# Four token blocks of a feed-forward part taken as two of 512 tokens, with their x fetched earlier and output products moved ahead

## The chip, the cores and the metric

One Trainium2 chip, one of its cores. The metric is the time on the device of one execution, in microseconds (us). Before the change it is 745.0 us, the median of 3 runs (744.06 to 746.33).

## The reference

Three parts, one after the other, on 2304 tokens (4 sequences of 576) of width 512. Cut to what matters here:

```python
# 1: attention in a window of 64 keys, 8 heads of 64
# 2: a dense feed-forward part, 512 -> 2048 -> 512
h = x @ w_in
sp = np.where(h > 20.0, h, np.log1p(np.exp(np.minimum(h, 20.0))))
g = h * np.tanh(sp)
x = g @ w_out
# 3: each token to one expert of 8, 512 -> 1024 -> 512
logits = x @ w_gate + modality_bias[modality_id]
e_idx = np.argmax(logits, axis=1)
...
for e in range(E):
    mask = e_idx == e
    h = np.maximum(x[mask] @ w1[e], 0.0)
    out[mask] = gate_w[mask, None] * (h @ w2[e])
```

The change is in part 2, and in what hands its rows on to part 3.

## The kernel before

**Tiles.** Part 2 takes the tokens in 9 blocks of 256. Every operand of a product is split into a rounded high part and a low part (hi + lo), and a product is three: hi x hi, lo x hi, hi x lo. `hidden` (line 341) makes 256 of the 2048 hidden features for one block: 2 halves of 128 features, 4 slices of the width, 3 products, so 24 TensorE products of 256 columns (tokens) into one bank of `h`. `mish_a`, `mish_b` and `split_g` turn `h` into `g`: on ScalarE a tanh (line 425), a square (426), an exp (427), a scaled copy (428), another square (436) and the rounded copy of g (444); on VectorE lines 430, 437, 438 and the low part of g (445). `output` (380) multiplies g with `w_out`: 12 products of 512 columns (features of the result) into the two banks of `acc`, one for each 128 tokens.

**The list of steps.** `steps` holds one entry for each step: ("m", block, feature group) for part 2, then ("s", slot, group) for expert slots of 256 tokens. The position i in it is used throughout: 0 to 15 are blocks 0 and 1, 16 to 23 block 2, then 8 positions for each block, 64 to 71 for block 8, and slots from 72. The loop at line 1221 writes out the order of every engine's queue by hand. In position i: the hidden products of i; the end of the activations of i-1 (`finish_mish`); a call of `run_tasks`; splits and fetches of x; the output products of i-2 (`LAG` is 2); the start of the activations of i (`start_mish`, its four ScalarE instructions); the split of g of i-1 (`finish_split`); a second call of `run_tasks`; and, where a block has ended, the copy of its two banks of `acc` into SBUF rows (`keep_rows`, a stash of 4 pairs). Up to position 27 attention's steps are woven in (`att_a`, `att_b`): products for scores and transposes behind the hidden products, products with v at the end.

**x.** Blocks from 2 on get x from DRAM: `fetch_x` (393) issues two transfers on SP in the fifth step of the block before; `split_x` (400) makes hi (ScalarE, line 407) and lo (VectorE, line 408), two instructions each, one step later. xh and xl have two buffers each, so the next block's x is written while the present one is read.

**Routing.** From position 28 on each `run_tasks` call takes one small task from a list. For each block there are 8 with two dot products each on VectorE (line 560), one that chooses the expert, an empty one, and one that places the rows: small TensorE products (line 611 and on), short VectorE instructions, and two scatters of rows to DRAM on POOL (line 639). Blocks are routed in order, 11 calls each, two calls a step; block 8 in a shorter form. When block 6 has been placed, two gathers on POOL (line 890) for the first slot follow, one in each of the second and third next call; position 71 transposes these rows on TensorE (`turn`, line 913).

Of the kernel before, what the change touches and what calls it, by code (L numbers as in the profile page):

```python
# [11 lines left out]
F32 = mybir.dt.float32  # L12
F32R = mybir.dt.float32r
BF16 = mybir.dt.bfloat16
I32 = mybir.dt.int32
# [24 lines left out]
PRE = 12  # L40
AHEAD = 1
MASK_PE = 26
PT_ACT = range(5, 27)
RAW_AT = -1, 1, 3
V_AT = 1
# [233 lines left out]
class Rounds:  # L279


    def __init__(self, nc, ctx, tc, a):
        self.nc, self.tc, self.ctx = nc, tc, ctx
        self.a = a
        self.c = {}
        self.s1, self.s2, self.x01 = [], [], {}
# [54 lines left out]
    def hidden(self, w, xh, xl):  # L341
# [49 lines left out]


    def fetch_x(self, b):
        self.xraw = []
        for i in range(2):
            t = self.x_pool.tile([P, 2, G], F32, name="xraw")
            self.nc.sync.dma_start(t, self.a["x"][b, :, 2 * i : 2 * i + 2])
            self.xraw.append(t)

    def split_x(self):  # L400

        nc = self.nc
        xh = self.xs_pool.tile([P, KD, G], F32R, name="xh")
        xl = self.xs_pool.tile([P, KD, G], F32R, name="xl")
        for i in range(2):
            to = slice(2 * i, 2 * i + 2)
            nc.scalar.copy(xh[:, to], self.xraw[i])
            nc.vector.tensor_tensor(xl[:, to], self.xraw[i], xh[:, to].bitcast(F32), ALU.subtract)
        return xh, xl

    def first_x(self, b):

        if b not in self.x01:
            self.x01[b] = (
                self.xs_pool.tile([P, KD, G], F32R, name="xh"),
                self.xs_pool.tile([P, KD, G], F32R, name="xl"),
            )
        return self.x01[b]

    def mish_a(self, h):  # L420
# [39 lines left out]
    def route_consts(self):  # L460
# [15 lines left out]
        tmp = room("row0")  # L476

        def iota(name, n, step, base=0, cm=0, dt=F32):
            i = p.tile([P, n], I32, name=name + "_i")
# [23 lines left out]
        def bias():  # L503
            n = NT // P
            mod = tmp(2 * n).bitcast(I64)
            nc.sync.dma_start(mod, self.a["mod"])
            mf = tmp(n)
            nc.vector.tensor_copy(mf, mod.bitcast(I32).rearrange("p (n t) -> p t n", t=2)[:, 0])
            b = p.tile([P, NM, NE], F32, name="brow")
# [12 lines left out]
            c["bias"] = bias  # L522
# [19 lines left out]

        return first, bias, last

    def keep_rows(self, acc, pool):

        rows = [pool.tile([P, ROW], F32, name=f"row{c}") for c in range(2)]
        for c in range(2):
# [357 lines left out]
    def turn(self, rows):  # L906
        nc = self.nc
        xh = self.xs_pool.tile([P, KD, G], F32R, name="xh")
        xl = self.xs_pool.tile([P, KD, G], F32R, name="xl")
# [33 lines left out]
def tile_kernel(tc, a):  # L943
    nc = tc.nc
    with ExitStack() as ctx:
# [7 lines left out]
        c0_pool = pool("consts", 1)  # L953
        R.w1_pool = pool("w1", 8)
        R.w2_pool = pool("w2", 8)
        R.xs_pool = pool("xsplit", 2)
        R.m_pool = pool("mish", 2)
        R.m1_pool = pool("mish1", 1)
        R.g_pool = pool("g", 3)
        c = R.c  # L960
        c["ident"] = c0_pool.tile([P, P], F32, name="ident")
        make_identity(nc, c["ident"])
# [5 lines left out]
        with tc.manual_schedule():  # L968
# [136 lines left out]
            gs, accs, xsp = {}, {}, {}  # L1105

            NS = EARLY + STRAIGHT
            steps += [("m", b, j) for b in range(2, NG) for j in range(FP)]
# [28 lines left out]
            def route_block(b, r):  # L1137
# [6 lines left out]
                tasks.append([choose])  # L1144
                if b in REST:
                    tasks.append([])
                tasks.append([weigh, place])
                routed.append(b)
                if len(routed) == PICK_AFTER + 1:
                    tasks[-1].append(R.pick)  # L1150
# [15 lines left out]

                    tasks.extend(([both], [], [others]))

            routed = []

            def out_step(i):
                if i < 0:
                    return
                part, b, j = steps[i]
                if j == 0:
                    accs[part, b] = new_acc(1 if b == NS - 1 else 2)
                last = (FP if part == "m" else FS) - 1
# [6 lines left out]
                if part == "s":  # L1184
                    R.finish(acc, rows.pop(b))
                else:
                    ended.append((b, acc))

            kept, waiting, late, ended = [], [], [], []
            pend, mish = None, None  # L1190
            end_convert = CONV_END
            n = len(steps)
# [13 lines left out]

            def start_mish():
                nonlocal mish
                if part == "m":
                    mish = R.mish_a(h)  # L1210

            def run_tasks():
# [8 lines left out]
            for i in range(n + LAG):  # L1221
                part, b, j = steps[i] if i < n else (None, None, None)
                if i == end_convert:
                    assert not todo and not half_done and not low_parts
                    early.close()
                    R.stash_pool = pool("stash", 4, side="right")
                    R.x_pool = pool("xraw", 2, side="right")
                if part == "m":
                    assert {("in", j, 0), ("in", j, 1)} <= ready
                if part:  # L1230
                    xh, xl = R.x01[b] if part == "m" and b < 2 else xsp[part, b]
                    if b < NS - 1:
                        h = R.hidden(R.w1[j] if part == "m" else ew1[b, j], xh, xl)
# [8 lines left out]
                if part == "s" and b < NS - 1:  # L1242
                    gs[i] = R.relu(h)
                turning = i >= TURN_AT
                if not turning:
                    run_tasks()
                if part == "m":
                    nxt = 2 if i == end_convert else b + 1 if b >= 2 and j == 4 else None
                    if nxt is not None and nxt < NG:
                        R.fetch_x(nxt)  # L1250
                    nxt = 2 if (b, j) == (1, FP - 1) else b + 1 if b >= 2 and j == 5 else None
                    if nxt is not None and nxt < NG:
                        xsp["m", nxt] = R.split_x()
                    if b == NG - 1:
                        if j == 0:
                            e0 = nc.values_load(
# [6 lines left out]
                            ew1[0, j - 6] = R.split_w1(j - 6)  # L1263
                        if j == 7:
                            assert len(rows[0]) == 2
                            xsp["s", 0] = R.turn(rows[0])
                            R.stage_tile(2)
                            R.fetch_w(e0, None, 2, 0)
                if part == "s" and b + 1 < EARLY and j == 1:
                    xsp["s", b + 1] = R.turn(rows[b + 1])  # L1270
                if part == "s" and j == 3 and EARLY <= b + 1 < NS:
                    xsp["s", b + 1] = R.turn(rows[b + 1])
# [49 lines left out]
            for s in range(STRAIGHT, NSLOT):  # L1322
# [8 lines left out]
                xh, xl = R.turn(r)  # L1331
                acc = new_acc()
                g = {}
                for k in range(FS + 1):
# [42 lines left out]
```

## Time and profile before

| | |
|---|---|
| median of 3 runs | 745.0 us (744.06 to 746.33) |
| the profiled execution | 745.39 us, of which 743.7 us from its first to its last instruction (span) |
| mean granted TensorE clock | 0.995 |
| DMA, mean over the span | 102 GB/s |
| positions 24 to 55 (blocks 3 to 6) | 229.63 to 415.98 us of the span |
| positions 56 to 71 (blocks 7 and 8) | 415.98 to 507.42 us |

Times of rows are us from the start of the span. In the timeline a row is start, duration, engine, line of the kernel, operation, out <- in, shape (partitions x elements), count, and in brackets the idle time of the engine before it with what released it. PE is TensorE, DVE VectorE, ACT ScalarE, POOL GpSimd, SP SyncE. TensorE products overlap, so what one costs in a run is the distance from its start to the next start, not its duration.

### The profile page before, as it was taken

To read this page: it belongs to the slowest core of one execution; us is meant where nothing else is said; L and a number is where in the kernel's file an instruction comes from. 1 tells how busy PE (TensorE), PEld (TensorE's weight loads), DVE (VectorE), ACT (ScalarE), POOL (GpSimd) and SP (SyncE) were. 2 spreads that over 40 slices of the span, in tenths; PEclk is the share of its full clock that TensorE was granted. 3 is DMA by queue.
4 is the path that set the end of the run, shared out by engine and by line. 5 is a ranking of instruction groups with operands and counts; after the bars stand their busy time and mean duration, and the time that the engine had idled before them with its cause. 6 is when DMAs were issued, how large, how long until landed. Compare 5 with 4: busy or idle time off the path is not lost. (4 is left out here: it accounts for less than half of the span.)

```text
span 743.7 us, 14036 instructions
## 1 busy us (share of the span) xinstructions
PE 719.8 (97%) x5123; PEld 648.3 (87%) x5123; DVE 558.7 (75%) x1316; ACT 496.4 (67%) x1036; POOL 154.5 (21%) x291
## 2 busy tenths in 40 slices
PE   5789999999999999999999999999999999999996
PEld 4678889889889899989998899998999999999995
DVE  4879999965565489888998898999987556545660
ACT  4978888888776677777767777776324546545462
POOL 4752232233223010100101001031123012220111
PEclk9999999999999999999999999999999999999998
DMA  9987677532332300100101000361012711110520
GB/s 263 308 237 220 198 239 225 183 107 79 94 109 70 128 31 1 49 10 30 58 1 58 1 30 29 114 172 56 30 57 72 255 43 58 57 44 29 200 85 33
DMA packets 42913, 75.51 MB, mean 102 GB/s; under 512 B 3858, under 2 KB 20242, under 8 KB 42707
## 3 DMA queue, kind: packets, MB, share of 16 engines
q1 hardware_dynamic: 30818, 56.01, 24.0%
q0 software_dynamic: 4480, 14.46, 5.7%
q10 hardware_dynamic: 7536, 4.06, 1.9%
q8 instruction: 42, 0.69, 0.4%
q14 instruction: 37, 0.30, 0.1%
HBM read 82.36 MB, written 13.39 MB: 129 GB/s over the span
## 5 line engine op out<-in xcount | busy, mean ns | idle before, releaser
L348 PE MATMUL h<-xh,w 128*128 128x256 f32 x576 | 166.8, 290 | 0.7 <-DVE y L438 0.7
L351 PE MATMUL h<-xl,w 128*128 128x256 f32 x576 | 163.5, 284 | 0.0
L352 PE MATMUL h<-xh,w 128*128 128x256 f32 x576 | 163.5, 284 | 0.0
L387 PE MATMUL acc<-w,g 128*128 128x512 f32 x288 | 115.6, 401 | 0.0
L348 PEld LDWEIGHTS h<-xh,w 128*128 128x128 f32 x576 | 110.9, 193 | 5.1 <-DVE y L438 1.2
L388 PE MATMUL acc<-w,g 128*128 128x512 f32 x288 | 112.6, 391 | 0.0
L389 PE MATMUL acc<-w,g 128*128 128x512 f32 x288 | 112.4, 390 | 0.0
L351 PEld LDWEIGHTS h<-xl,w 128*128 128x128 f32 x576 | 111.0, 193 | 1.5
L352 PEld LDWEIGHTS h<-xh,w 128*128 128x128 f32 x576 | 110.9, 193 | 0.0
L560 DVE CUSTOM_DVE_ANT_0 junk<-row,wg 128x512 bf16<-128x512 f32 x144 | 99.2, 689 | 2.7
L452 ACT ACTIVATE g<-h 128x512 fp32r<-128x512 f32 x36 | 21.5, 598 | 93.6 <-PE h L352 78.6
L425 ACT ACTIVATE y<-h 128x512 f32<-128x512 f32 x72 | 43.1, 599 | 59.6 <-PE h L352 56.5
L351 PE MATMUL h<-xl,ew 128*128 128x256 f32 x288 | 81.6, 283 | 0.6 <-DVE xl L918 0.6
L352 PE MATMUL h<-xh,ew 128*128 128x256 f32 x288 | 81.5, 283 | 0.0
L348 PE MATMUL h<-xh,ew 128*128 128x256 f32 x288 | 81.5, 283 | 0.0
L211 POOL TENSOR_SCALAR p<-p,r 128x128 f32<-128x128 f32 x144 | 68.8, 495 | 58.4 <-DVE r L204 55.0
L430 DVE SCALAR_TENSOR_TENSOR pq<-y,r 128x512 f32<-128x512 f32 x72 | 49.6, 689 | 29.0 <-ACT r L428 29.0
L436 ACT ACTIVATE pq<-pq,mid 128x512 f32<-128x512 f32 x72 | 52.2, 725 | 23.7 <-DVE pq L430 19.5
L639 POOL DMA_INDIRECT xs_dram<-row,posi x18 | 19.5, 1081 | 227.5 <-DVE row L630 92.2
L389 PEld LDWEIGHTS acc<-w,g 128*128 128x128 f32 x288 | 54.1, 188 | 12.1 <-DVE g L445 0.2
L445 DVE TENSOR_TENSOR g<-y,g 128x512 fp32r<-128x512 f32 x72 | 49.4, 687 | 17.8 <-ACT g L444 17.7
L387 PEld LDWEIGHTS acc<-w,g 128*128 128x128 f32 x288 | 54.3, 188 | 9.1
(219 smaller groups left out, 1645.8 us busy)
## 6 DMA issues: line engine op xcount, KB each, us to landing
s<-e_w SPq DMA_DIRECT2D x32, 1024.0 KB
v<-v SPq DMA_DIRECT2D x36, 256.0 KB
raw<-w_in SPq DMA_DIRECT2D x16, 512.0 KB
raw<-w_out SPq DMA_DIRECT2D x16, 512.0 KB
kt<-kT SPq DMA_DIRECT2D x17, 384.0 KB
qd<-qT SPq DMA_DIRECT2D x36, 128.0 KB
x_dram<-xs ACTq DMA_DIRECT2D x14, 256.0 KB
xraw<-x_dram SPq DMA_DIRECT2D x14, 256.0 KB
```

The source lines that it names most:

```text
L211: nc.gpsimd.tensor_scalar(p[:, c, :], p[:, c, :], r[:, c : c + 1], 0.0, ALU.mult, ALU.add)
L348: nc.tensor.matmul(h[:, f], w[:, 0, k, fs], xh[:, k], start=(k == 0), stop=False)
L351: nc.tensor.matmul(h[:, f], w[:, 0, k, fs], xl[:, k], start=False, stop=False)
L352: nc.tensor.matmul(h[:, f], w[:, 1, k, fs], xh[:, k], start=False, stop=(k == KD - 1))
L387: nc.tensor.matmul(acc[c], gh[:, 0, f, cs], w[:, 0, f], start=st, stop=False)
L388: nc.tensor.matmul(acc[c], gh[:, 0, f, cs], w[:, 1, f], start=False, stop=False)
L389: nc.tensor.matmul(acc[c], gh[:, 1, f, cs], w[:, 0, f], start=False, stop=en)
L425: nc.scalar.activation(y, h, AF.Tanh, scale=0.5)
L430: nc.vector.scalar_tensor_tensor(p, y, 1.0, r, ALU.add, ALU.mult)
L436: nc.scalar.activation(p, p, AF.Square, bias=self.c["mid"][:, 0:1])
L445: lo_engine.tensor_tensor(flat(t[:, 1]), g, flat(t[:, 0]).bitcast(F32), ALU.subtract)
L560: nc.vector.tensor_tensor_reduce(out=junk, in0=rows[c][:, 0:D], in1=self.wg[:, e], scale=1.0, scalar=0.0, op0=ALU.mult, op1=ALU.add, accum ...
```

## The change

- Blocks 3 and 4, and 5 and 6, are taken together. A wide step ("w", block, f) makes 128 hidden features for 512 tokens: 12 products of 512 columns (`hidden_wide`), and 12 output products into four banks of `acc` (`output_wide`). Positions 24 to 39 are blocks 3 and 4, 40 to 55 blocks 5 and 6; the number of positions stays.
- x lives in one buffer of 512 tokens; a 256-token block takes its half (odd blocks the second). Where both halves are in use, the next x can be written only when the last hidden products of the present step have read them.
- x is fetched in step 10 of a wide pair's 16 (in step 3 for the first pair), into 4 buffers in place of 2, and split in the last step: four ScalarE copies and four VectorE subtractions at position 39, two and two at 23 and 55.
- `changes` holds positions 23, 39 and 55. In the position behind each, the output products of i-2 come before the hidden products of i. In the positions themselves the first call of `run_tasks` is left out.
- The rows of wide pairs are copied from `acc` by ScalarE and VectorE, one bank each; both blocks of a pair end at once, the first block (third and fourth bank) is copied first. The stash has 3 pairs of rows in place of 4, and a copy starts only when fewer than 3 are held.
- Some small constants share room with other tiles.

```diff
+WIDE = 3, 5
+    def hidden_wide(self, w, f, xh, xl):
+        nc = self.nc
+        h = self.h_ps.tile([P, 2, G], F32, name="h").rearrange("p f t -> p (f t)")
+        fs = slice(f * P, (f + 1) * P)
+        for k in range(KD):
+            nc.tensor.matmul(h, w[:, 0, k, fs], xh[:, k], start=(k == 0), stop=False)
+            nc.tensor.matmul(h, w[:, 0, k, fs], xl[:, k], start=False, stop=False)
+            nc.tensor.matmul(h, w[:, 1, k, fs], xh[:, k], start=False, stop=(k == KD - 1))
+        return h
+    def output_wide(self, acc, gh, w, f, first, last):
+        nc = self.nc
+        gh = gh.rearrange("p x f t -> p x (f t)")
+        for c in range(4):
+            cs = slice(c * P, (c + 1) * P)
+            nc.tensor.matmul(acc[c], gh[:, 0, cs], w[:, 0, f], start=first, stop=False)
+            nc.tensor.matmul(acc[c], gh[:, 0, cs], w[:, 1, f], start=False, stop=False)
+            nc.tensor.matmul(acc[c], gh[:, 1, cs], w[:, 0, f], start=False, stop=last)
...
+    def split_wide(self, b, blocks):
+        nc = self.nc
+        for i in range(2):
+            to = slice(2 * i, 2 * i + 2)
+            for n in blocks:
+                xh, xl = self.parts_x(n % 2)
+                raw = self.xraw.pop((n, i))
+                nc.scalar.copy(xh[:, to], raw)
+                nc.vector.tensor_tensor(xl[:, to], raw, xh[:, to].bitcast(F32), ALU.subtract)
+        return self.parts_x()
...
-            self.nc.scalar.activation(rows[c][:, 0:D], acc[c], AF.Copy, scale=2.0)
+        self.nc.scalar.activation(rows[0][:, 0:D], acc[0], AF.Copy, scale=2.0)
+        if shared:
+            self.nc.vector.tensor_scalar(rows[1][:, 0:D], acc[1], 2.0, None, ALU.mult)
+        else:
+            self.nc.scalar.activation(rows[1][:, 0:D], acc[1], AF.Copy, scale=2.0)
...
+                if part == "w":
+                    if j == 0:
+                        assert not ended
+                        accs[part, b] = new_acc() + new_acc()
+                    last = 2 * FP - 1
+                    acc = accs[part, b]
+                    R.output_wide(acc, gs.pop(i), R.w2[j // 2], j % 2, j == 0, j == last)
+                    if j == last:
+                        ended.extend(((b + 1, acc[:2], True), (b, acc[2:], True)))
+                    return
...
-                    R.stash_pool = pool("stash", 4, side="right")
-                    R.x_pool = pool("xraw", 2, side="right")
+                    R.stash_pool = pool("stash", 3, side="right")
+                    R.x_pool = pool("xraw", 4, side="right")
...
-                if part:
+                changed = i - 1 in changes
+                if changed:
+                    out_step(i - LAG)
+                if part == "w":
+                    h = R.hidden_wide(R.w1[j // 2], j % 2, *xsp[part, b])
+                elif part:
...
-                if not turning:
+                if not turning and i not in changes:
                     run_tasks()
+                if part == "w" and j == 10:
+                    R.fetch_x(b + 2)
+                    if b + 2 in WIDE:
+                        R.fetch_x(b + 3)
+                if part == "w" and j == 2 * FP - 1:
+                    if b + 2 in WIDE:
+                        xsp["w", b + 2] = R.split_wide(b + 2, (b + 2, b + 3))
+                    else:
+                        xsp["m", b + 2] = R.split_x(b + 2)
...
-                out_step(i - LAG)
+                if not changed:
+                    out_step(i - LAG)
...
-                if ended:
-                    b0, acc = ended.pop()
-                    rows0 = b0, R.keep_rows(acc, R.stash_pool)
+                while ended and stashed - len(routed_out) < 3:
+                    stashed += 1
+                    b0, acc, shared = ended.pop()
+                    rows0 = b0, R.keep_rows(acc, R.stash_pool, shared)
```

## Rows read from the trace of the kernel before

**Rows 1.** The page's part 1: busy time, share of the span and instructions.

```profile
PE 719.8 (97%) x5123; PEld 648.3 (87%) x5123; DVE 558.7 (75%) x1316; ACT 496.4 (67%) x1036; POOL 154.5 (21%) x291
```

**Rows 2.** Waits of TensorE from 290 to 545 us: total, times, longest.

```profile
PE h L351 <- DVE xl L918: 0.6, 1, 0.6
PE h L348 <- DVE y L438: 0.4, 2, 0.2
PE t L611 <- DVE xl L918: 0.2, 1, 0.2
```

**Rows 3.** Timeline of TensorE over position 36.

```profile
302.07 0.28 PE L348 MATMUL h<-xh,w 128*128 128x256 f32 x1
...
304.94 0.40 PE L387 MATMUL acc<-w,g 128*128 128x512 f32 x1
...
305.41 0.39 PE L389 MATMUL acc<-w,g 128*128 128x512 f32 x1
...
307.46 0.39 PE L389 MATMUL acc<-w,g 128*128 128x512 f32 x1
307.69 0.28 PE L348 MATMUL h<-xh,w 128*128 128x256 f32 x1
```

**Rows 4.** Timeline of all engines, end of position 34 and start of 35.

```profile
293.70 0.60 ACT L425 ACTIVATE y<-h 128x512 f32<-128x512 f32 x1 [0.83 <-PE h L352]
...
296.25 0.28 PE L348 MATMUL h<-xh,w 128*128 128x256 f32 x1
...
296.29 0.61 ACT L444 CAST g<-y 128x512 fp32r<-128x512 f32 x1
...
297.03 0.68 DVE L445 TENSOR_TENSOR g<-y,g 128x512 fp32r<-128x512 f32 x1
```

**Rows 5.** Timeline: row copies of a block, then an x split.

```profile
291.19 1.08 ACT L549 ACTIVATE row<-acc 128x512 f32<-128x512 f32 x2
...
401.04 1.12 ACT L407 CAST xh<-xraw 128x512 fp32r<-128x512 f32 x2
...
404.98 1.29 DVE L408 TENSOR_TENSOR xl<-xraw,xh 128x512 fp32r<-128x512 f32 x2
```

**Rows 6.** Timeline of three engines, positions 23 and 24, beside attention.

```profile
225.01 0.60 ACT L425 ACTIVATE y<-h 128x512 f32<-128x512 f32 x1 [1.36 <-PE h L352]
...
226.10 0.48 PE L387 MATMUL acc<-w,g 128*128 128x512 f32 x1
...
226.39 0.69 DVE L226 COPY pt<-t 128x512 f32<-128x512 f32 x1 [1.13 <-PE t L221]
...
229.14 0.60 ACT L444 CAST g<-y 128x512 fp32r<-128x512 f32 x1
...
229.63 0.39 PE L348 MATMUL h<-xh,w 128*128 128x256 f32 x1
...
229.78 0.69 DVE L445 TENSOR_TENSOR g<-y,g 128x512 fp32r<-128x512 f32 x1 [1.25 <-ACT g L444]
```

**Rows 7.** Timeline: block 6 is placed, scattered, gathered and transposed, positions 68 to 71.

```profile
486.72 0.18 PE L611 MATMUL t<-oh,tri 128*128 128x8 bf16 x1
...
490.26 1.00 POOL L639 DMA_INDIRECT xs_dram<-row,posi  x1 [0.19 <-ACT g L444]
...
496.80 1.42 POOL L890 DMA_INDIRECT grow<-xs_dram,idx  x1 [5.53 <-DVE g L445]
498.53 1.01 POOL L890 DMA_INDIRECT grow<-xs_dram,idx  x1 [0.30 <-issue]
...
503.78 1.03 PE L913 MATMUL t<-ident,grow 128*128 128x128 f32 x8
```

**Rows 8.** Landing times: scatters of the whole run (median), gathers from 480 to 520.

```profile
xs_dram<-row,posi POOLq DMA_INDIRECT x18, 3.8
...
DMA to landing us min/median/max: 3.4/3.7/4.6
```

More of the change, by code (lines that the diff above doesn't have):

```diff
@@ L397, in fetch_x, with parts_x, split_x @@
             self.nc.sync.dma_start(t, self.a["x"][b, :, 2 * i : 2 * i + 2])
-            self.xraw.append(t)
-    def split_x(self):
+            self.xraw[b, i] = t
+    def parts_x(self, half=None):
+        if half is None:
+            return self.x[:, 0], self.x[:, 1]
+        ts = slice(half * G, (half + 1) * G)
+        return self.x[:, 0, :, ts], self.x[:, 1, :, ts]
+    def split_x(self, b):
         nc = self.nc
-        xh = self.xs_pool.tile([P, KD, G], F32R, name="xh")
-        xl = self.xs_pool.tile([P, KD, G], F32R, name="xl")
+        xh, xl = self.parts_x(b % 2)
         for i in range(2):
             to = slice(2 * i, 2 * i + 2)
-            nc.scalar.copy(xh[:, to], self.xraw[i])
-            nc.vector.tensor_tensor(xl[:, to], self.xraw[i], xh[:, to].bitcast(F32), ALU.subtract)
+            raw = self.xraw.pop((b, i))
+            nc.scalar.copy(xh[:, to], raw)
+            nc.vector.tensor_tensor(xl[:, to], raw, xh[:, to].bitcast(F32), ALU.subtract)
         return xh, xl
-    def first_x(self, b):
[L413 to L417, printed above, removed]
+    def split_wide(self, b, blocks):
[5 more added lines that the diff above has]
+                raw = self.xraw.pop((n, i))
+                nc.scalar.copy(xh[:, to], raw)
+                nc.vector.tensor_tensor(xl[:, to], raw, xh[:, to].bitcast(F32), ALU.subtract)
+        return self.parts_x()
+    def first_x(self, b):
+        self.x01[b] = self.parts_x(b % 2)
         return self.x01[b]
@@ L478, in iota @@
         def iota(name, n, step, base=0, cm=0, dt=F32):
-            i = p.tile([P, n], I32, name=name + "_i")
+            i = p.tile([P, n], I32, name=name) if dt == I32 else tmp(n).bitcast(I32)
             nc.gpsimd.iota(i, [[step, n]], base=base, channel_multiplier=cm)
@@ L543, in route_consts, with keep_rows @@
         return first, bias, last
-    def keep_rows(self, acc, pool):
+    def keep_rows(self, acc, pool, shared):
         rows = [pool.tile([P, ROW], F32, name=f"row{c}") for c in range(2)]
-        for c in range(2):
-            self.nc.scalar.activation(rows[c][:, 0:D], acc[c], AF.Copy, scale=2.0)
+        self.nc.scalar.activation(rows[0][:, 0:D], acc[0], AF.Copy, scale=2.0)
[3 more added lines that the diff above has]
+            self.nc.scalar.activation(rows[1][:, 0:D], acc[1], AF.Copy, scale=2.0)
         return rows
@@ L904, in gather_slot, with turn @@
         return [self.gather(idx, 2 * s + t) for t in range(1 if s == STRAIGHT - 1 else 2)]
-    def turn(self, rows):
+    def turn(self, rows, half):
         nc = self.nc
-        xh = self.xs_pool.tile([P, KD, G], F32R, name="xh")
-        xl = self.xs_pool.tile([P, KD, G], F32R, name="xl")
+        xh, xl = self.parts_x(half)
         for t in range(len(rows)):
@@ L1107, in tile_kernel @@
             NS = EARLY + STRAIGHT
-            steps += [("m", b, j) for b in range(2, NG) for j in range(FP)]
+            for b in range(2, NG):
+                if b in WIDE:
+                    steps += [("w", b, f) for f in range(2 * FP)]
+                elif b - 1 not in WIDE:
+                    steps += [("m", b, j) for j in range(FP)]
             steps += [("s", s, k) for s in range(NS) for k in range(FS)]
@@ L1146, in route_block @@
                     tasks.append([])
-                tasks.append([weigh, place])
+                tasks.append([weigh, place, lambda: routed_out.append(b)])
                 routed.append(b)
@@ L1167, in route_block @@
                     tasks.extend(([both], [], [others]))
-            routed = []
+            routed, routed_out = [], []
+            changes = {
+                i
+                for i in range(len(steps) - 1)
+                if steps[i + 1][0] == "w" and steps[i + 1][2] == 0
+                or steps[i][0] == "w" and steps[i + 1][0] == "m"
+            }
             def out_step(i):
@@ L1186, in out_step @@
                 else:
-                    ended.append((b, acc))
-            kept, waiting, late, ended = [], [], [], []
+                    ended.append((b, acc, False))
+            kept, waiting, late, ended, stashed = [], [], [], [], 0
             pend, mish = None, None
@@ L1208, in start_mish @@
                 nonlocal mish
-                if part == "m":
+                if part in ("m", "w"):
                     mish = R.mish_a(h)
@@ L1244, in tile_kernel @@
                 turning = i >= TURN_AT
-                if not turning:
+                if not turning and i not in changes:
                     run_tasks()
-                if part == "m":
[L1248 to L1253, printed above, removed]
+                if part == "w" and j == 10:
[7 more added lines that the diff above has]
+                        xsp["m", b + 2] = R.split_x(b + 2)
+                if part == "m":
+                    if i == end_convert:
+                        R.fetch_x(2)
+                    if (b, j) == (1, FP - 1):
+                        xsp["m", 2] = R.split_x(2)
+                    if b + 1 in WIDE:
+                        if j == 3:
+                            R.fetch_x(b + 1)
+                            R.fetch_x(b + 2)
+                        if j == 5:
+                            R.split_x(b + 1)
+                        if j == FP - 1:
+                            xsp["w", b + 1] = R.split_wide(b + 1, (b + 2,))
+                    elif b >= 2 and b + 1 < NG:
+                        if j == 4:
+                            R.fetch_x(b + 1)
+                        if j == 5:
+                            xsp["m", b + 1] = R.split_x(b + 1)
                     if b == NG - 1:
@@ L1265, in tile_kernel @@
                             assert len(rows[0]) == 2
-                            xsp["s", 0] = R.turn(rows[0])
+                            xsp["s", 0] = R.turn(rows[0], 1)
                             R.stage_tile(2)
@@ L1269, in tile_kernel @@
                 if part == "s" and b + 1 < EARLY and j == 1:
-                    xsp["s", b + 1] = R.turn(rows[b + 1])
+                    xsp["s", b + 1] = R.turn(rows[b + 1], b % 2)
                 if part == "s" and j == 3 and EARLY <= b + 1 < NS:
-                    xsp["s", b + 1] = R.turn(rows[b + 1])
-                out_step(i - LAG)
+                    xsp["s", b + 1] = R.turn(rows[b + 1], b % 2)
+                if not changed:
+                    out_step(i - LAG)
                 if turning:
```

10 lines of the change are left out of this document (5 added, 5 removed).

## Prediction

> **What bounds the kernel now.** The page's busy line comes first: TensorE is busy 97% of the span, VectorE and ScalarE 75% and 67% [rows 1]. Busy time alone would not settle it, so the waits of TensorE come next, over the stretch from block 4 to the first expert slots: in 255 us it waits 0.4 us for VectorE to release a bank of h and 0.6 us for the x of the first expert slot [rows 2]. So in the changed stretch TensorE sets the time, and nothing else is late. The timeline of one plain step (position 36) gives the unit: 24 hidden products of 256 columns from 302.07 to 304.94 (2.87 us, 0.120 each), 12 output products of 512 columns to 307.69 (2.75 us), together 5.62 us [rows 3]. Every added wait of TensorE is therefore paid in full, and every product cadence saved is earned in full, until the last step of block 8.
>
> The other thing to see is how little room the output products have. At the start of position 35 (296.25) ScalarE only begins the rounded copy of g for position 33, VectorE finishes the low part at 297.71 [rows 4]. That costs nothing now, because a step begins with 2.87 us of hidden products and the output products come behind them.
>
> **Wider products: the gain.** 32 narrow steps (positions 24 to 55) become 32 wide ones: 24 + 12 products become 12 + 12, all of 512 columns. Inside a run the 512-column products follow each other at 0.228 us (305.41 to 307.46, nine intervals) [rows 3]; two of 256 take 0.240. I take 24 x 0.228 = 5.47 us for a wide step: 0.15 saved, 32 x 0.15 = 4.8 us. A hidden product of 512 columns is not in the trace. Bounds: at 0.240 the gain is nothing; at 0.225 it is 32 x 12 x 0.015 = 5.8. The nearest row is the output product of the same shape, so 4.8. A loss is excluded, since no product needs a load that it did not need before.
>
> The Trainium skill speaks against this gain ("TensorE: Matmul & The Clock Gate", section "Back-to-back issue gap"): warm products follow at N / 2.4 GHz plus about 2.5 ns. By that rule two of 256 columns cost only 2.6 ns more than one of 512, and 384 such pairs give an estimated 1.0 us in place of 4.8. The trace doesn't agree: it has 120 ns for 256 columns where the rule has 109.
>
> **Output products first at positions 24, 40 and 56: the cost.** Here the output products of position i-2 stand ahead of the hidden products of i, so g of i-2 is needed at the very start of the step, when, as said, it isn't there. The new x copies make it later: they stand in ScalarE's queue ahead of the four activations on h of i-1, and these ahead of the copy of g. An x copy is 0.55 us, its subtraction 0.65 [rows 5].
>
> Position 40 (512 to 512 tokens, four copies). Count from the start of the tanh on the finished h [rows 4]: the next step starts 2.55 us later (296.25 - 293.70), the copy of g ends at 3.20, its low part at 4.01. Two of the four copies touch only the first half of x, which TensorE has read before its hidden products end, so I let them run early; two (1.1 us) fall behind h. High part then at 4.3, low part at 5.1. TensorE waits 1.8 us, does two products (0.46), waits about 0.4 again: 2.2 us. Bounds: 1.1 with no copy in the way, 3.3 with all four.
>
> Position 41. Since nothing lies between the hidden products of 40 and of 41, the output products of 39 come 2.74 - 0.3 = 2.4 us after h of 40 in place of 5.4; g of 39 stands behind the activations of 40, ready at 3.2 and 4.0. Wait 0.8 + 0.3 = 1.1 us (0 to 2).
>
> Position 42. All four banks of acc belonged to blocks 3 and 4, and the next block needs them all (before, two pairs alternated). Block 4's rows are copied out last, though its banks are needed first, and its stash buffer is that of block 1, whose scatter is still under way: by my count of task calls block 1 is placed in this same position 41. From place to the issue of the second row's scatter took 3.54 us (486.72 to 490.26), landing 3.8 in the median [rows 7, 8]; with VectorE's 0.7 for the copy the bank is free 8.0 us after the place. TensorE asks for it after the wait 1.1, output 2.75, hidden 2.74 and three products 0.68: 7.3. Wait 0.8; 0 if the scatter lands in 3.0, 3.5 if it takes the 6.5 that lie between 490.26 and 496.80.
>
> Position 56 (512 to 256, two copies, one of them early): 0.55 us behind h, high part at 3.75, low part at 4.56: 1.25 + 0.35 = 1.6 us (1.1 to 2.2). Position 57 like 41, with 2.88 us of hidden products: 1.0 (0 to 2).
>
> Position 24, still beside attention. ScalarE runs without a gap from the tanh (225.01) to the end of the copy of g (229.74) [rows 6]; two x copies shift that by 1.1 to 230.85. Output products are wanted at 229.63: 1.25, and 0.25 more for the low part. Later in that step attention's transposes and the products with v now stand next to each other, without output products between; VectorE's copy ends at 227.08, where the next product behind the transposes could start at 226.10 [rows 6]: 1.0. Together 2.5 us (1.0 to 3.5).
>
> **Routing one step later.** Two task calls are left out (positions 39 and 55; the one at 23 finds no task), and there are two calls a step. Counting calls, block 6 is placed in position 69 in place of 68, block 8 in 78 in place of 77. In the trace the place of block 6 (486.72) is followed by its scatters, by the two gathers for the first slot (496.80 and 498.53, the second landing 3.4 to 4.6 later, 501.9 to 503.1) and by the transposes that read them in position 71 (503.78) [rows 7, 8]. Room: 0.7 to 1.9 us. A step less (5.62, with block 6's place 5.7) makes this a wait of 3.8 to 5.0 us. The scatter waited behind a weight transfer: 6.5 us from its issue to the gather, 3.8 in the median; without that the wait is 2.1 to 2.7 less. The second weight transfer is issued in just the step that the place moves to, so I take 3.8, bounds 1 to 5. The 0.8 us that the same slot's x costs now (0.6 and 0.2 [rows 2]) goes, since VectorE catches up meanwhile: -0.8. Block 8's table also comes a step later; its first reader is at position 83, more than a step away, so nothing.
>
> **At no cost.** The x transfers: no row of TensorE waits for one, five steps earlier or not; on SP nothing urgent is queued behind them before block 8. Row copies on VectorE: four move from ScalarE (0.54 each [rows 5]) to VectorE (about 0.7), counted at position 42. If VectorE has no room there, they show as h released late; the 0.4 us of that kind in the stretch [rows 2] I take as gone, as the wide x needs fewer splits in mid-block (0 to -1). The edits of constants and pools only save room.
>
> **Sum.** -4.8 - 0.4 + 2.5 + 2.2 + 1.1 + 0.8 + 1.6 + 1.0 + 3.8 - 0.8 = +7.0 us. The profiled execution took 745.39 us (span 743.7 and 1.7 around it), 0.4 above the median 745.0 of the runs, so 752.4 beside the profile and 752.0 beside the median.
>
> **Rivals.**
> 1. The waits vanish and the wide products pay (faster). Place: the three x changes. If ScalarE got x and g done inside the 2.75 us of output products, the order would cover the x split as written, and if the gathers land as fast as the fastest row the transposes lose little: 745 - 4.8 - 0.4 = 739.8. It decides once all waits together stay under 5.2 us. For it: ScalarE is busy only 67% [rows 1]. Against: the copy of g is late already without any x copy [rows 4].
> 2. A draw. The waits at their lower bounds (1.0 + 1.1 + 0.5 + 1.1 + 0.5 = 4.2), routing 1.0: 745 - 5.2 + 5.2 = 745. For it: every upper half of my terms rests on queues that I have placed by reading the code.
> 3. Worse. x is now one buffer; if the copies wait for all its readers (1.1 at position 40, 0.5 at 56), the scatter at position 42 takes 6.5 (2.7) and the gathers 5.0 (1.2): 752 + 5.5 = 757.5. For it: VectorE has little room in this stretch, and two waits on it show [rows 2].
> 4. The wide hidden products follow at 0.2375 us, hardly faster than two of 256 columns (0.240): the gain is 12 x 32 x 0.0025 = 1.0 us, the rest as forecast, 752 + 3.8 = 755.8. Against it: the output products of the same shape at 0.228 [rows 3]. The page of the Trainium skill named above would have a gain of that size.
>
> **Chances.** Forecast 0.56, rival 1 0.13, rival 2 0.14, rival 3 0.14, rival 4 0.03. The forecast's own range is 748 to 755.5. The range for 8 in 10 goes from 744, which leaves rival 1 out, to 757. 0.3% is 2.2 us, about what a measurement tells from no change. Faster by more: rival 1, 0.13. Within: rival 2 and the low end of the forecast, 0.15. Slower: 0.72.
>
> **What would show it.** Timeline of TensorE: wide steps of 5.47 us between position 43 and 54; a gap before the first output product of positions 24, 40, 56, released by the copy of g (ScalarE) and then by its low part (VectorE); a gap at the first output product of position 42, released by a row copy; a gap before the transposes of position 71, released by a gather. Waits of TensorE in sum about 13 us from position 24 to 71. The forecast is wrong if the gaps at 24, 40 and 56 are under 1 us each, if x and not g is what ends them, or if wide steps are not 5.4 to 5.5 us.

## The result and the profile after

The changed kernel takes 751.73 us in the median of 4 runs (750.58 to 754.06). The kernel before, run beside it, took 744.53 (743.84 to 746.33). The ratio is 1.0098, with an interval from 1.0079 to 1.0117: about 7.2 us slower. The forecast was 752.0.

The profiled execution took 750.58 us, its span is 748.9 (before 743.7), the mean granted clock 0.997 (before 0.995), so the clock explains nothing of it. What ran before position 23 differs by 1 or 2 us from one execution to the next (position 23 starts at 221.84 before and 220.42 after; from 53 to 57 us TensorE's granted clock is 0.57 before and 1.00 after), therefore positions are compared from 23 on. A position's time is the distance from the start of its hidden products to the next. From position 23 to 74 the kernel before takes 299.14 us, the changed one 305.58: +6.44.

The page's part 1, after:

```profile
PE 717.4 (96%) x4739; PEld 626.9 (84%) x4739; DVE 561.0 (75%) x1320; ACT 495.2 (66%) x1032; POOL 159.3 (21%) x291
```

Against [rows 1], TensorE has 384 products less and is busy 2.4 us less in a span that is 5.2 us longer. So TensorE isn't slower, it waits. The waits of TensorE from 220 to 520 us (waiting instruction, what it waited for, us in total, times, longest):

```profile
PE acc L375 <- ACT g L480: 3.5, 4, 1.6
PE t L951 <- DMA grow<-xs_dram,idx: 2.4, 2, 1.2
PE acc L375 <- DVE row L586: 1.9, 2, 1.3
PE o L238 <- DVE pt L227: 0.8, 1, 0.8
PE acc L409 <- ACT g L480: 0.6, 1, 0.6
PE h L364 <- DVE y L474: 0.4, 1, 0.4
PE h L349 <- DVE y L474: 0.2, 1, 0.2
```

In [rows 2] there were four small waits. Now there are 12, 9.8 us in sum: five for the rounded copy of g, two for the first slot's gathers, two for a bank of `acc` that VectorE has still to copy out, the others small. The modelled duration of a product covers part of a gap behind it, so a short wait can be missing here. It shows in the same view of the weight loads (PEld), where the low part of g appears too:

```profile
PEld acc L375 <- ACT g L480: 4.7, 4, 2.0
...
PEld acc L377 <- DVE g L481: 2.1, 4, 0.5
```

A plain wide step (timeline of TensorE, position 36):

```profile
300.56 0.39 PE L364 MATMUL h<-x,w 128*128 128x512 f32 x1
300.78 0.39 PE L365 MATMUL h<-x,w 128*128 128x512 f32 x1
...
303.28 0.39 PE L375 MATMUL acc<-w,g 128*128 128x512 f32 x1
...
306.00 0.39 PE L364 MATMUL h<-x,w 128*128 128x512 f32 x1
```

It is 306.00 - 300.56 = 5.44 us for 24 products, 0.227 each, against 5.62 in [rows 3]. The hidden part takes 2.72 (24 products of 256 columns took 2.87).

Positions 39 and 40, from the timeline of all engines (dots stand for lines left out):

```profile
318.44 1.14 ACT L447 CAST x<-xraw 128x512 fp32r<-128x512 f32 x2
...
319.80 1.14 ACT L447 CAST x<-xraw 128x512 fp32r<-128x512 f32 x2 [0.22 <-PE h L366]
...
320.84 0.59 ACT L461 ACTIVATE y<-h 128x512 f32<-128x512 f32 x1
...
323.42 0.60 ACT L480 CAST g<-y 128x512 fp32r<-128x512 f32 x1
...
324.07 0.50 PE L375 MATMUL acc<-w,g 128*128 128x512 f32 x1 [1.59 <-ACT g L480]
324.15 0.69 DVE L481 TENSOR_TENSOR g<-y,g 128x512 fp32r<-128x512 f32 x1
...
324.41 0.40 PE L376 MATMUL acc<-w,g 128*128 128x512 f32 x1
...
324.89 0.50 PE L377 MATMUL acc<-w,g 128*128 128x512 f32 x1
```

Two of the four x copies run early, two wait for the last hidden product and hold back the tanh (320.84). The copy of g ends at 324.0, and with it the first wait of TensorE; the third product, the first to read the low part, comes 0.48 us behind the second in place of 0.23. In [rows 4] the same copy ended after the next step's start too (296.90 against 296.25), but 2.87 us of hidden products stood in between.

VectorE's row copies and TensorE in position 42:

```profile
340.11 0.69 DVE L586 TENSOR_SCALAR row<-acc 128x512 f32<-128x512 f32 x1
...
340.85 0.50 PE L375 MATMUL acc<-w,g 128*128 128x512 f32 x1 [0.61 <-DVE row L586]
...
343.02 0.69 DVE L586 TENSOR_SCALAR row<-acc 128x512 f32<-128x512 f32 x1 [2.22 <-DMA xs_dram<-row,posi]
...
343.76 0.50 PE L375 MATMUL acc<-w,g 128*128 128x512 f32 x1 [1.26 <-DVE row L586]
```

There are two waits, one at each pair of banks. The second row copy has to wait 2.22 us for the scatter of block 1, whose stash buffer it takes.

Block 6 is placed, scattered, gathered and transposed:

```profile
496.00 0.18 PE L650 MATMUL t<-oh,tri 128*128 128x8 bf16 x1
...
499.52 1.01 POOL L678 DMA_INDIRECT xs_dram<-row,posi  x1 [0.19 <-issue]
...
504.74 1.57 POOL L929 DMA_INDIRECT grow<-xs_dram,idx  x1 [4.21 <-DVE l L599]
506.61 1.48 POOL L929 DMA_INDIRECT grow<-xs_dram,idx  x1 [0.30 <-issue]
...
508.77 0.66 PE L951 MATMUL t<-ident,grow 128*128 128x128 f32 x4 [1.16 <-DMA grow<-xs_dram,idx]
...
510.62 0.63 PE L951 MATMUL t<-ident,grow 128*128 128x128 f32 x4 [1.19 <-DMA grow<-xs_dram,idx]
```

The place has moved from position 68 to 69; where [rows 7] had the transposes as one run of 8 without a wait, each half now waits for its gather.

### The profile page after: what moved, and what is told of

The parts are those of the page before. It is cut to its first block, busy times and chain, and to the rows that moved or that the text cites. A ratio compares the mean times of both kernels' runs of the same rounds, so it can differ in the third digit from the quotient of the medians.

```text
span 748.9 us, 13253 instructions
## 1 busy us (share of the span) xinstructions
PE 717.4 (96%) x4739; PEld 626.9 (84%) x4739; DVE 561.0 (75%) x1320; ACT 495.2 (66%) x1032; POOL 159.3 (21%) x291
## 5 line engine op out<-in xcount | busy, mean ns | idle before, releaser
L349 PE MATMUL h<-x,w 128*128 128x256 f32 x320 | 93.1, 291 | 0.6 <-DVE y L474 0.6
L352 PE MATMUL h<-x,w 128*128 128x256 f32 x320 | 90.5, 283 | 0.0
L353 PE MATMUL h<-x,w 128*128 128x256 f32 x320 | 90.5, 283 | 0.0
L353 PE MATMUL h<-x,ew 128*128 128x256 f32 x288 | 81.5, 283 | 0.0
L349 PE MATMUL h<-x,ew 128*128 128x256 f32 x288 | 81.5, 283 | 0.0
L352 PE MATMUL h<-x,ew 128*128 128x256 f32 x288 | 81.5, 283 | 0.0
L409 PE MATMUL acc<-w,g 128*128 128x512 f32 x160 | 65.1, 407 | 0.6 <-ACT g L480 0.6
L349 PEld LDWEIGHTS h<-x,w 128*128 128x128 f32 x320 | 61.2, 191 | 3.2 <-DVE y L474 1.1
L411 PE MATMUL acc<-w,g 128*128 128x512 f32 x160 | 62.6, 392 | 0.0
L410 PE MATMUL acc<-w,g 128*128 128x512 f32 x160 | 62.5, 391 | 0.0
L352 PEld LDWEIGHTS h<-x,w 128*128 128x128 f32 x320 | 61.3, 192 | 0.5
L353 PEld LDWEIGHTS h<-x,w 128*128 128x128 f32 x320 | 61.3, 191 | 0.0
L409 PE MATMUL acc<-ew,g 128*128 128x512 f32 x152 | 60.6, 399 | 0.0
L410 PE MATMUL acc<-ew,g 128*128 128x512 f32 x152 | 59.6, 392 | 0.0
```

What stands on the lines that cost most here:

```text
L349: nc.tensor.matmul(h[:, f], w[:, 0, k, fs], xh[:, k], start=(k == 0), stop=False)
L352: nc.tensor.matmul(h[:, f], w[:, 0, k, fs], xl[:, k], start=False, stop=False)
L353: nc.tensor.matmul(h[:, f], w[:, 1, k, fs], xh[:, k], start=False, stop=(k == KD - 1))
L409: nc.tensor.matmul(acc[c], gh[:, 0, f, cs], w[:, 0, f], start=st, stop=False)
L410: nc.tensor.matmul(acc[c], gh[:, 0, f, cs], w[:, 1, f], start=False, stop=False)
L411: nc.tensor.matmul(acc[c], gh[:, 1, f, cs], w[:, 0, f], start=False, stop=en)
```

## The experiments

The theory: the gain of the wide products is there, and two things give back more than it, the output products moved ahead and the routing that comes a step later. A chip ran the kernel before beside each group of kernels (medians 745.09 for the first four, 744.08 for the next four, 744.5 for the last). Ratios are to it.

**Hidden products first everywhere.** In the changed kernel:

```diff
-                changed = i - 1 in changes
+                changed = False
```

> The changed kernel with its hidden products first everywhere, as before the change; all else stays. Theory (the waits at positions 24, 40, 41, 56 and 57 come from asking for g before it exists): these five waits go, 1.9 + 2.2 + 1.2 + 1.7 + 1.4 = 8.4 us in the trace of after, so about 743.3 us, and TensorE waits neither for g nor for x there. Rival (the x split needs the cover of the output products): waits for x of about the same size come in their place, 749 us or more.

Measured: 744.69 us (742.92 to 747.45, 12 runs), ratio 1.0001 [0.9988, 1.0014]. The theory holds. The waits of TensorE from 215 to 522 us in this kernel:

```profile
PE t L951 <- DMA grow<-xs_dram,idx: 2.4, 2, 1.2
PE acc L375 <- DVE row L586: 1.2, 1, 1.2
PE h L364 <- DVE y L474: 0.4, 1, 0.4
```

No wait for g is left, none beside attention, and none for x, whose split these positions still hold. By the ratios the order costs 0.0097 x 745 = 7.2 us, all that the change costs. One of the row waits went with it: position 42 takes 7.45 in place of 8.40. So the output products moved ahead protected nothing. The profiled execution (743.19 us) is among the shorter of the 12; in it positions 23 to 74 take 296.50 us, 2.6 less than in the kernel before. The longest (747.45) has a mean granted clock of 0.990 in place of 0.994, so over the 12 executions part of that gain goes with the clock.

**The order alone, in the kernel before.**

```diff
+                if i in (24, 40, 56):
+                    out_step(i - LAG)
...
-                out_step(i - LAG)
+                if i not in (24, 40, 56):
+                    out_step(i - LAG)
```

> The kernel before, all blocks of 256 tokens, x split in mid-block as it was; only the output products of i-2 stand ahead of the hidden products at positions 24, 40 and 56. Theory (the order alone costs, since g is copied only at the start of a step): waits of about 1.1 us at 40 and 56, about 1 us at 41 and 57, 1.4 us at 24: about 750 us. Rival (only the x copies make g late): the time stays within 1 us of the kernel before, 745.

Measured: 751.30 us (750.63 to 753.36, 6 runs), ratio 1.009 [1.0077, 1.0104]. The order costs 6.7 us also with blocks of 256 tokens, where x is split two positions before the block's end and no x copy is near: positions 23 and 24 take 1.3 more, 39 to 41 2.4 more (19.53 against 17.09), 55 to 57 2.6 more (19.76 against 17.15). So the x copies can be only the smaller part of the price.

**The split of g earlier in the queues.** In the changed kernel, the order kept:

```diff
                     finish_mish()
+                if i in changes or changed:
+                    finish_split()
```

> The changed kernel with its order of products kept; at positions 23, 39, 55 and the one behind each, the split of g is written right behind the end of its activations, ahead of the x copies and of the activations of the next h. Theory (ScalarE's queue order is what makes g late): no wait for g at 24, 40, 41, 56, 57; the 0.8 us wait for attention's transposed values at 24 stays; 744 to 745 us. Rival (output products ahead cost by their place in TensorE's order, whatever g does): 750 us or more.

Measured: 751.70 us (749.12 to 752.99, 6 runs), ratio 1.0089 [1.007, 1.0107]. The theory missed here: no wait for g is left, and the time has not moved. ScalarE in position 39 of this kernel, and then TensorE at the start of position 41's hidden products:

```profile
319.96 0.62 ACT L480 CAST g<-y 128x512 fp32r<-128x512 f32 x1 [2.55 <-DVE y L474]
320.49 2.18 ACT L447 CAST x<-xraw 128x512 fp32r<-128x512 f32 x4
322.57 0.59 ACT L461 ACTIVATE y<-h 128x512 f32<-128x512 f32 x1
```

```profile
328.70 0.50 PE L364 MATMUL h<-x,w 128*128 128x512 f32 x1 [1.89 <-DVE y L474]
```

The copy of g now stands ahead of all four x copies, and waits itself 2.55 us for its input. So all four copies fall behind h, the tanh starts 6.81 us after the start of position 39 (322.57 - 315.76) in place of 3.96 (320.84 - 316.88), and the chain from it to VectorE's last instruction on h releases the bank too late for the hidden products two steps on. Waits of this kind make 3.9 us in the stretch (0.6 before the edit): one wait had turned into another. That isn't all of it. Positions 23 and 24, 39 to 41 and 55 to 57 together still take 2.8 us less than without the edit; of this position 42 gives back 0.9 (9.29 in place of 8.40; the waits for row copies are 2.6 us, before the edit 1.9), position 71 gives back 0.5, and position 43 gives back 1.6 (7.20 in place of 5.56). There the granted clock is 0.50 from 345 to 348 us, behind these waits, where the changed kernel has 1.00.

**The same early split without x copies near.** On the kernel of the order alone, right behind the end of the activations:

```diff
+                if i in (23, 24, 39, 40, 55, 56):
+                    finish_split()
```

> The kernel before with output products first at positions 24, 40 and 56 (blocks of 256 tokens, no split of x in these steps), and in positions 23, 24, 39, 40, 55 and 56 the split of g is put into the queues of ScalarE and VectorE right behind the end of the activations of the step before, ahead of the four activations of the newest h. It asks why the same early split of g turned the wait into one for h in the kernel with wide blocks. Theory: the copies and subtractions of x did that, since they stood between g and the tanh on the newest h; here there are none, so the waits for g go and no wait for h comes: steps 39 to 41 take about 17.1 us (19.53 without the early split, 17.09 before), steps 55 to 57 about 17.2 (19.76; 17.15), position 24 keeps about 1 us of its cost beside attention; time 745.5 to 747. Rival: the order is too short for either chain by itself; g no longer waits, but the hidden products of 41 and 57 wait for VectorE's last instruction on h by 1 us or more each, and the time stays at 749 or above (751.3 without the early split).

Measured: 746.86 us (746.3 to 749.91, 8 runs), ratio 1.0042 [1.0026, 1.0058]: inside the theory's range, and by the ratios 3.6 us less than the order alone. The waits of TensorE's products name g no more, and one for h of some size shows, ahead of the hidden products of position 42 (the rival had it at 41 and 57):

```profile
337.14 0.35 PE L348 MATMUL h<-xh,w 128*128 128x256 f32 x1 [0.58 <-DVE y L438]
```

Positions 39 to 41 take 18.02 and 55 to 57 18.23: of the 2.4 and 2.6 us, 0.9 and 1.1 are left (the theory had 0.0 and 0.1). The weight loads show what the products' view hides, short waits for g, two of them in position 55:

```profile
417.40 0.19 PEld L387 LDWEIGHTS acc<-w,g 128*128 128x128 f32 x1 [0.48 <-ACT g L444]
...
418.13 0.19 PEld L389 LDWEIGHTS acc<-w,g 128*128 128x128 f32 x1 [0.43 <-DVE g L445]
```

So the queue order of g makes over half of the price of the order when no x copies are there. With them, in both orders that were tried, one of the two demands on ScalarE stays late: g for the output products, or the tanh for the release of h.

**No task call left out.** In the changed kernel, the order kept:

```diff
-                if not turning and i not in changes:
+                if not turning:
```

> The changed kernel without leaving out a task call at positions 23, 39 and 55. Theory (the wait at 71 comes from the two calls): block 6 is placed in position 68 again, the 2.8 us at position 71 go and the 1.4 us that 72 and 73 had gained come back; two dot products more stand ahead of the x subtractions at 39 and 55, and the low part of g at 40 and 56 comes up to 1.4 us later each. In sum 750 to 751.5 us, and no wait for a gather at 71. Rival (the wait at 71 has another cause, the weight transfers): it stays.

Measured: 759.89 us (757.35 to 762.27, 6 runs), ratio 1.02 [1.0177, 1.0223]. A miss, by 8 us. The wait for the gathers stayed (1.97 and 1.10 us), because block 6 was placed only at the end of position 68, and its second scatter was issued at 501.48, 1.3 us behind a weight transfer of 1 MB (500.18). The DMA issues from 494 to 512 us (count, median us from issue to landing):

```profile
xs_dram<-row,posi POOLq DMA_INDIRECT x2, 7.7
```

That is 7.7 us in place of 3.8 in the run's median before [rows 8]. Second, positions 39 and 55 wait longer, now also for the low part of g on VectorE (1.24 and 1.00 us). And TensorE's clock fell. Busy times in four stretches (length, then busy us and instructions of each engine, granted clock, DMA share, GB/s):

```profile
418.00:422.00 4.00, 1.92 (x8) 0.92 (x7) 3.93 (x11) 2.25 (x4) 0.00 (x0) 0.98 0.00 0
422.00:425.00 3.00, 3.00 (x9) 2.33 (x8) 2.93 (x16) 0.00 (x0) 0.00 (x0) 0.50 0.00 0
425.00:428.00 3.00, 3.00 (x25) 2.96 (x24) 0.26 (x2) 0.00 (x0) 0.00 (x0) 0.96 0.00 0
...
514.00:520.00 6.00, 4.90 (x15) 4.03 (x15) 4.37 (x9) 4.17 (x7) 4.08 (x4) 0.50 0.66 173
```

After a stretch in which TensorE had work for 1.92 of 4 us, the granted clock is 0.50 (1.2 of 2.4 GHz) for 3 us, and products follow at 0.43 us (422.39 to 422.82) in place of 0.227. The second time it lasts some 7 us from 514 (0.51 from 514 to 521), behind the wait for the gathers. At half speed these 10 us do the work of 5, so up to an estimated 5 us of the 8 are the clock's. Both stretches stand right behind waits longer than those of the changed kernel, where the clock stayed up; that the waits brought them on is likely, but no run changes the one without the other.

**Two calls left out, in the kernel before.**

```diff
-                if not turning:
+                if not turning and i not in (39, 55):
```

> The kernel before, blocks of 256 tokens; only the first task call of positions 39 and 55 is left out. Theory: block 6 is placed in position 69, the transposes of position 71 wait 2.5 to 4 us for a gather, of which 72 and 73 give back up to 1.4: 746.5 to 747.5 us. Rival (the wait at 71 needs the other waits ahead of it): 745.1 us.

Measured: 746.02 us (744.39 to 748.24, 12 runs), ratio 1.002 [1.0007, 1.0032], +1.5 us. Block 6 is placed at 490.20 in position 69, TensorE waits 1.21 and 1.11 us for the two gathers, and position 71 takes 10.83 (6.51 before). Behind these waits the granted clock is 0.51 from 505 to 508, so up to an estimated 1.5 us of position 71 is the clock's in this execution. Positions 72 and 73 give 1.5 of it back and the waits at 52 to 55 are gone. The mechanism stands, at 1.5 us net when alone.

**The step given back in another way.** In the changed kernel, the order and the left-out calls kept; the empty call is taken from blocks 0, 5 and 6:

```diff
-REST = range(NG)
+REST = 1, 2, 3, 4, 7, 8
```

> The changed kernel with its order of products kept, and the empty task left out for blocks 0, 5 and 6. Theory: as there, the waits at 71 and for the stash at 42 go, the waits for g stay: about 749 us. Rival (crowded DMA queues): 751.7 us.

Measured: 749.58 us (748.6 to 750.89, 6 runs), ratio 1.0065 [1.005, 1.008]. The wait for the gathers is gone (position 71 takes 6.51 as before) and the one for row copies fell from 1.9 to 0.8; those for g stay (3.4 and 0.6). The scatters of block 6 stand right behind a weight transfer here too (491.18 behind 491.16) and land after 8.2 and 8.8 us, but the block is placed at 487.87, at the end of position 67, and the gathers are in time. So a crowded queue alone doesn't make the wait: it takes a late place too. The empty call was of some use: without it position 62 takes 6.63 in place of 5.76 in the kernel before, with a wait of 0.62 for VectorE's choice of the expert.

**Hidden products first, and the step given back.** Both edits together:

> Hidden products first everywhere, and the empty task left out for blocks 0, 5 and 6, so that by count block 1 is placed at the end of position 40 and block 6 at the end of 67. Theory (what is left of the waits comes from the two task calls: the gather at 71, and the scatter of block 1 that still holds a stash buffer at 42): both waits go, 2.8 and about 1.5 us, and the 1.4 us that 72 and 73 gain by the wait come back: about 741.5 us, faster than both kernels. Rival (they come from the crowded DMA queues): both stay, 744.7 us.

Measured: 740.18 us (739.17 to 741.6, 5 runs), ratio 0.9943 [0.9928, 0.9958], faster than both kernels. Its waits of TensorE from 215 to 522 us:

```profile
PE h L352 <- DVE x L956: 1.0, 1, 1.0
PE t L650 <- DVE oh L635: 0.5, 1, 0.5
PE h L364 <- DVE y L474: 0.2, 1, 0.2
```

This is the time of rival 1 of the prediction (739.8), though not by its mechanism: there the order was to cover the x split, here it is undone. The wide products pay once neither g nor the gathers are late.

**Hidden products first, and no call left out.** The edits of the first and of the fifth experiment together:

> Hidden products first everywhere and no task call left out. Two dot products more stand ahead of the x subtractions at 39 and 55 (1.4 us of VectorE), so the last part of x comes up to 1.2 us late at 40 and less at 56; block 6 is placed at the end of position 68, half a step earlier than in the changed kernel. Theory: the wait at 71 then depends on whether its scatter falls behind the second weight transfer: 743 to 747 us, slower than the version without the three empty tasks. Rival (a call left out protects nothing): 742 us or less.

Measured: 747.11 us (746.25 to 750.47, 8 runs), ratio 1.0038 [1.0022, 1.0053], just above what was expected. Without the gap in the calls, x is late: one hidden product of position 40 and one of 56 waits for VectorE's subtractions, 0.9 us each. The scatters again stand right behind a weight transfer (489.47 behind 489.44) and land after 7.8 us, position 71 takes 12.85, and the clock shows 0.61 from 505 to 512. Against the first experiment position 40 takes 1.4 and position 56 1.2 us more. So leaving out the calls protects the x split by some 2 us, and the empty calls are the better place to take the time from.

## Why the prediction was right, and where its terms were off

Differences of positions after minus before; a wide step is counted as 0.18 cheaper than a narrow one.

| term | forecast, us | measured, us |
|---|---|---|
| 32 wide steps | -4.8 | 32 x (5.62 - 5.44) = -5.8 |
| waits for h in positions 52 to 55 | -0.4 | 23.42 - 4 x 5.62 = -0.9 |
| position 24, beside attention | +2.5 | 17.26 - 15.58 + 0.18 = +1.9 |
| 39 and 40 | +2.2 | 13.13 - 2 x 5.44 = +2.2 |
| 41 | +1.1 | 6.67 - 5.44 = +1.2 |
| 42 | +0.8 | 8.40 - 5.44 = +3.0 |
| 55 and 56 | +1.6 | 12.78 - 5.44 - 5.62 = +1.7 |
| 57 | +1.0 | 7.00 - 5.62 = +1.4 |
| 71, routing | +3.8 | 9.28 - 6.51 = +2.8 |
| 72 and 73 | -0.8 | 12.14 - 13.56 = -1.4 |
| sum | +7.0 | +6.1 |

The measured terms add up to 6.1; the other positions make the 6.44 of the whole (58 alone has +0.3, mostly the small products of a placing that stood in 57 before).

- **What bounds the kernel** was right: TensorE, with almost no wait. That is why each new wait showed in the time.
- **Wide products.** The mechanism was right, the size was at the upper bound: hidden products of 512 columns follow at 0.227 us. The rule that was weighed against it there (the Trainium skill, "TensorE: Matmul & The Clock Gate", section "Back-to-back issue gap", which gives it for a single product by itself and not for a stream of products with a weight load each, as here) would have a spacing of 216 ns and a gain of an estimated 1.0 us; the trace agrees with neither.
- **g at positions 40, 41, 56 and 57.** Where the waits stand, what ends them and their sizes came out within 0.4 us. At position 40 the high part cost 1.75 (forecast 1.8), counted from the last product before (322.09) less its cadence; the rest of the 2.2 is the low part and the slower start of the first products (forecast 0.4). The share of the x copies was too high: with no x copy near, in the order-alone run, 39 and 40 already lose 1.4 us and 55 and 56 lose 1.8, so the copies carry 0.8 at 40 (forecast 1.1) and nothing at 56 (forecast 0.55), where the size was right by luck. The runs with the early split show that the reason is the queue as a whole, not the place of g alone. At position 24 the wait for g is 0.62 (forecast 1.25 and 0.25), and the one for attention's transposed values 0.78 (forecast 1.0).
- **Position 42** is the term with the wrong step. "Block 4's rows are copied out last, though its banks are needed first" fails: the first output product of 42 takes its bank without a wait, as the banks were given out in the order in which they came free, and the waits are at 340.85 and 343.76. What I missed is VectorE's row copy of the first pair, which ran behind two dot products and was a wait of its own. The stash buffer held by block 1's scatter was right (2.22 us), but the chain to it was longer: from the place (332.74) to the second scatter's issue (338.46) 5.7 us in place of 3.54, and to the free bank (343.71) 11.0 in place of 8.0. TensorE asks for that bank last of the four and not second, which hides part of it. A wait of 0.36 for h behind it (345.08) is in the term too. In all 3.0 in place of 0.8, inside the bound of 3.5.
- **Routing.** The step that the place moves by, the queue and the wait at 71 were right, and two experiments show both directions: two calls left out in the kernel before, and the step given back in the changed one. The size was 1.0 too high: the first scatter went out 2.1 us behind the second weight transfer (498.25 behind 496.19) and landed in 4.7 us, where the two of the kernel before took 5.9 in the median; from the second scatter to the gather there are 5.2 us (6.5 in [rows 7]).
- **The return.** I had only the 0.8 of position 72; with it position 73 gave back 0.5 more, together 1.4.
- Errors of -1.0 (gain), +2.2 (42), -1.0 (71) and -0.6 (return) nearly cancel, so that the time came out within 0.3 us is luck: the terms were not that good.
- **Two rivals.** In rival 2 the waits at 41 and 57 stand with 0.5 each, though their lower bounds are 0; with these the draw would be 744. Rival 3 needed all x copies to wait for the last reader of x; two of the four ran early (318.44).

Not tried: the wide kernel with output products first and its x split moved away from these positions, which would show whether the early split of g then pays there too.

## What to carry to other kernels

When the bounding engine waits for nothing, an order is worth as much as the time it leaves to the producers: count from the start of the last product on h to the finished g, and compare it with the work that stands between. Moving a producer earlier in its queue helps only if what it passes has room too, so ask which other wait its queue feeds (here the release of h). When a gain goes missing, undo the order and the moved calls apart: two one-line edits gave back all of it, and more than the change had cost.

## What the runs showed of the hardware that was not expected

- TensorE's granted clock was 0.50 behind waits of about 1 us: with no task call left out, from 422 to 425, after waits of 1.08 and 1.00 us and 1.92 us of work in 4 us, with products at 0.43 in place of 0.227 us; so these 2.1 us of waits came with an estimated 1.5 us more. The same stands behind waits of 1.24, 1.33 and 0.36 us in the changed kernel with the early split (345 to 348), and of 1.21 and 1.11 us with two calls left out in the kernel before (505 to 508). It isn't sure to come: in the changed kernel TensorE had work for 2.03 of the 4 us from 508 to 512, and the clock stayed at 1.00. The Trainium skill ("TensorE: Matmul & The Clock Gate", section "Part 1: The HAM clock gate (the "warmup" mystery)") has the throttled level as the default, which activity releases; of this the trace shows the two levels and the return while TensorE had work (0.96 from 425 to 428), not the default: the first 3 us of the kernel before, without any product, have 1.00.
- The two row scatters of block 6, issued within 1.3 us behind a weight transfer of 1 MB, landed after 7.5 to 8.8 us (four runs); issued 2.1 to 3.5 us behind one, after 4.5 to 6.1 (the other runs, with 5.9 in the median in the kernel before). The median of all scatters of the kernel before is 3.8.
